# Two chained MLPs behind an attention: the column order of the MLP matmuls

## The chip, the cores and the metric

The kernel runs on one core of one Trainium2 chip. The metric is the device time of one execution in microseconds, as the median of several runs. Of one execution there is a profile with a trace of every engine: TensorE (PE; its weight loads appear as PEld), VectorE (DVE), ScalarE (ACT), GpSimd (POOL) and SyncE (SP, which issues the DMAs).

## What is computed

An attention with a learned bias over 2 batches, 8 heads, 576 positions and head dimension 64, then two MLPs over the resulting 1152 tokens of width 512, with 2048 hidden units each. The change touches the MLPs alone:

```python
# x: (1152, 512), the attention's output, token by token
h = x @ w_in                                             # 1152 x 2048
g = np.where(h > 0.0, h, np.exp(np.minimum(h, 0.0)) - 1.0)
x = g @ w_out                                            # 1152 x 512
h = x @ w2_in
g = np.maximum(h, 0.0) + np.log1p(np.exp(-np.abs(h)))
return g @ w2_out
```

## The kernel before, in words

Every operand of an MLP product is held as a high and a low part in a rounded float32 format (`F32R`), and a product is three matmuls into one accumulator: high by high, high by low, low by high.

The 1152 tokens are cut into three chunks of 512, 256 and 384 columns (`CHS`), numbered 0, 1 and 2. Each MLP goes over them in two passes (`PASSES`): chunks 0 and 1 together, then chunk 2. Inside a pass the loop runs over the 16 blocks of 128 hidden units. One block and chunk is a tile with two groups of matmuls. `ffn1` (L1137) makes h: 4 pieces of the width of 512 times 3 products, 12 matmuls into one PSUM bank, with the weights stationary and the tokens (`xh`, `xl`) as the moving operand of 512, 256 or 384 columns (the matmul is L1146). ACT and DVE then turn h into g, split in `gh` and `gl`, from the tiles that `g_tiles` (L1132) hands out. `drain` (L1173) accumulates g times the second weight matrix: in the first MLP (m = 0) the weights are stationary and g moves, 12 matmuls to a tile; in the second (m = 1) g is stationary and the 512 columns of the weights move, 3 matmuls to each 128 tokens (the matmul is L1190). The accumulators lie in PSUM for all 16 blocks (`acc`, L1126).

Over both MLPs that is 1008 matmuls with 512 moving columns (384 of `ffn1`, 192 of the first MLP's `drain`, all 432 of the second's), 576 with 384 columns and 576 with 256 columns (in both cases 384 of `ffn1` and 192 of the first MLP's `drain`): 2160 matmuls and 884,736 columns. Each has its own weight load of 128 columns.

The weights come from HBM as 64-bit floats. DMA, ACT, POOL and DVE turn them into high and low parts (L148 to L187, the last step is the low part `wl` at L187), block by block while the MLP runs. A planner (`Order`) sets the order of the instructions on every engine from written costs and due times; the tables stand in `DUE` and `ON`. It runs when the program is built, and its inputs are not touched by the change.

In SBUF all MLP operands begin at the same place within 256 bytes, but for chunk 1: its `xh` and `xl` (`x_tiles`, L111), and its g in the first MLP, are shifted by `OFF` = 48 words, which is 192 bytes, inside tiles that are 64 words longer than needed.

Of the kernel before, what the change touches and what calls it, by code (L numbers as in the profile page):

```python
# [12 lines left out]
F32R = mybir.dt.float32r  # L13
# [7 lines left out]
P = 128  # L21
# [6 lines left out]
CHS = [512, 256, 384]  # L28
# [4 lines left out]
KT = DM // P  # L33
DFF = 2048
FT = DFF // P
# [10 lines left out]
PRK = 3  # L46

NE = 5


OFF = 48

NRAW, NWB = 3, 4
NF = (3, 4)
# [57 lines left out]
def x_tiles(ctx, tc, cs, xh, xl):  # L112
    pool = ctx.enter_context(tc.tile_pool(name=f"xp{cs[0]}", bufs=1, side="right"))
    for c in cs:
        for x, nm in ((xh, "xh"), (xl, "xl")):
            if c != 1:
                x.append(pool.tile([P, KT, CHS[c]], F32R, name=f"{nm}{c}"))
            else:
                t = pool.tile([P, KT * CHS[c] + 64], F32R, name=f"{nm}{c}")
                x.append(t[:, OFF : OFF + KT * CHS[c]].rearrange("p (k n) -> p k n", k=KT))  # L120


class Weights:
# [66 lines left out]
def attention(xctx, tc, qe, qt, kt, vt, par, tab, xh, xl, W, M):  # L190
    nc = tc.nc
    ctx = ExitStack()

    x_tiles(xctx, tc, [0], xh, xl)
    vctx = ExitStack()
    vr = vctx.enter_context(tc.tile_pool(name="vr", bufs=1, side="right")).tile([P, B * HP, 9, D], F32, name="vr")
# [480 lines left out]
    for p in VPARTS:  # L677
# [3 lines left out]
        t_v += [h, lo]  # L681
    t_v += vz
    t_open = add(None, 0, lambda e: (vctx.close(), x_tiles(xctx, tc, range(1, len(CHS)), xh, xl)), t_v, 3)

    tab1 = pack_table(1)
# [408 lines left out]
    return np.concatenate(rows)  # L1094


class Mlps:


# [30 lines left out]
        return self.ps2[:, k // 2, k % 2 * CHS[c] :][:, : CHS[c]] if m == 0 else self.ps2[:, k]  # L1130

    def g_tiles(self, m, c, f):  # L1132
        tag, n, bufs = ("gs", CHS[1] + 64, 2) if c == 1 else ("g", 512, 3)
        o = OFF if c == 1 and m == 0 else 0
        return [self.ap.tile([P, n], F32R, tag=f"{tag}{x}", name=f"g{x}{m}{c}{f}", bufs=bufs)[:, o : o + CHS[c]] for x in range(2)]

    def ffn1(self, m, c, f, slot):  # L1137

        nc, xh, xl = self.nc, self.xh, self.xl
        h, l = self.W.pairs[m, f][:2]  # L1140
        ch = CHS[c]
        ps = (self.left if slot else self.right).tile([P, 512], F32, tag="ph", name=f"ph{m}{c}{f}")[:, :ch]
        n = 0
        for kk in range(KT):
            for a, x in ((h, xh[c]), (h, xl[c]), (l, xh[c])):
                nc.tensor.matmul(ps, a[:, kk], x[:, kk], start=n == 0, stop=n == 3 * KT - 1)  # L1146
                n += 1
        g, t = [], []

        def act():  # L1150
            t.append(self.ap.tile([P, DM], F32, tag="t", name=f"t{m}{c}{f}", bufs=2)[:, :ch])
            if m == 0:
                nc.scalar.activation(t[0], ps, AF.Relu, scale=-1.0)
                nc.scalar.activation(t[0], t[0], AF.Exp, scale=-1.0)
            else:
                nc.scalar.activation(t[0], ps, AF.Abs)
                nc.scalar.activation(t[0], t[0], AF.Exp, scale=-1.0)
                nc.scalar.activation(t[0], t[0], AF.Ln, bias=1.0)  # L1158

        def both():  # L1160
            if m == 0:
                nc.vector.scalar_tensor_tensor(t[0], t[0], -1.0, ps, op0=ALU.add, op1=ALU.max)  # L1162
            else:
                nc.vector.scalar_tensor_tensor(t[0], ps, 0.0, t[0], op0=ALU.max, op1=ALU.add)  # L1164

        def hi():
            g.extend(self.g_tiles(m, c, f))
            nc.scalar.copy(g[0], t[0])  # L1168

        def lo():  # L1170
            nc.vector.tensor_sub(g[1], t[0], g[0])  # L1171

        return act, both, hi, lo, g  # L1173

    def drain(self, mcf, g, parts):
        m, c, f = mcf
        gh, gl = g
        h, l = self.W.pairs[m, f][2:]
        for j in parts:
            js = slice(j * P, (j + 1) * P)  # L1180
            if m == 0:
                prods = [(a[:, js], x) for a, x in ((h, gh), (h, gl), (l, gh))]
            else:
                prods = [(a[:, js], x) for a, x in ((gh, h), (gh, l), (gl, h))]

            two = m == 0 and c == 1
            if two and f == 0 and j % 2 == 0:
                self.nc.tensor.matmul(self.ps2[:, j // 2], self.zero, self.xh[0][:, 0], start=True, stop=False)
            for n, (a, x) in enumerate(prods):
                self.nc.tensor.matmul(  # L1190
                    self.acc(m, c, j), a, x, start=f == 0 and n == 0 and not two, stop=f == FT - 1 and n == 2 and not (two and j % 2 == 0)
                )

    def finish_hi(self, c, k):
# [87 lines left out]
```

## Time and profile before

| what | value |
|---|---|
| time, median of 3 runs | 603.33 us (602.89 to 603.76) |
| the profiled execution's own time | 604.67 us |
| its span, from first to last instruction | 602.9 us |
| PE busy | 581.3 us, 96% of the span, 5165 matmuls |
| PE's weight loads busy | 495.1 us |
| DVE busy | 438.2 us, 73% |
| ACT busy | 409.7 us, 68% |
| POOL busy | 111.1 us, 18% |
| mean granted clock of TensorE | 0.982 of 2.4 GHz |

The MLP's matmuls begin at 192.2 us in the span and the last starts at 597.6 us. A matmul's duration in the trace runs from its start to the end of its results, and matmuls are pipelined, so one starts long before the one ahead of it has ended; what a matmul costs in a full stream is the distance from its start to the next one's start, not its duration. The profiled execution is 1.34 us (0.2%) above the median of the three runs, and 1.77 us of its time lie outside the span.

### The profile page before, as it was taken

How to read it: one execution, taken by the hardware profiler on the slowest of the kernel's cores; microseconds unless marked ns; L12 is line 12 of the kernel's file. 1: busy time of each engine (PE TensorE's matmuls, PEld its weight loads, DVE VectorE, ACT ScalarE, POOL GpSimd, SP SyncE). 2: the span in 40 equal slices, each digit the busy share in tenths (PEclk: the TensorE clock that was granted, in tenths of full speed). 3: DMA queues.
4: the chain of work that ended last, by engine and by line, in shares of the span. 5: the costliest groups of instructions: out<-in, count | busy, mean ns of one | idle time of the engine just before them, and what ended most of it. 6: DMA issues, size and time to landing. Idle time of an engine off the chain costs nothing.

```text
span 602.9 us, 12979 instructions
## 1 busy us (share of the span) xinstructions
PE 581.3 (96%) x5165; PEld 495.1 (82%) x5165; DVE 438.2 (73%) x883; ACT 409.7 (68%) x833; POOL 111.1 (18%) x146
## 2 busy tenths in 40 slices
PE   7778999999999999999999999999999999999996
PEld 4445777777788888888899999998888888988985
DVE  7699999999889999999943379999994232233222
ACT  6686998989998867666633476679884455455442
POOL 2322474447600011011200012100010000000000
PEclk8779999999999999999999999999999999999999
DMA  8733643244300344344530004444530000011001
GB/s 324 210 100 80 201 115 99 77 116 144 86 23 2 119 146 157 119 160 143 172 106 1 1 30 146 155 129 137 171 109 0 2 0 1 1 41 64 1 1 53
DMA packets 19069, 56.39 MB, mean 94 GB/s; under 512 B 2112, under 2 KB 2496, under 8 KB 18752
## 3 DMA queue, kind: packets, MB, share of 16 engines
q1 hardware_dynamic: 19008, 55.56, 29.4%
q8 instruction: 40, 0.66, 0.4%
q14 instruction: 21, 0.17, 0.1%
HBM read 41.40 MB, written 2.36 MB: 73 GB/s over the span
## 4 chain that ended last, share of the span: by engine, by line
PE 81%; DVE 8%; ACT 2%; issue 2%; DMA 1%; DVEq 0%; ACTq 0%
PE ps L1190 33%; PE ph L1146 33%; PE tp L564 5%; PE pb L406 4%; PE pa L589 3%; PE ps L524 3%; DVE e L534 2%; DVE et L573 2%; DVE y L399 1%; ACT sg L418 1%; DMA sp<-sg 1%; DVE wl L187 0%; PE pr L619 0%; DVE xs L607 0%; ACT e L551 0%
## 5 line engine op out<-in xcount | busy, mean ns | idle before, releaser
L1146 PE MATMUL ph<-xh,wh 128*128 128x512 f32 (+2 forms) x384 | 129.0, 336 | 0.7 <-DVE t L1162 0.7
L1146 PE MATMUL ph<-xh,wl 128*128 128x512 f32 (+2 forms) x384 | 128.8, 335 | 0.0
L1146 PE MATMUL ph<-xl,wh 128*128 128x512 f32 (+2 forms) x384 | 128.7, 335 | 0.0
L1168 ACT CAST g<-t 128x256 fp32r<-128x256 f32 (+2 forms) x96 | 48.3, 512 | 75.7 <-PE ps L1190 68.7
L1171 DVE TENSOR_TENSOR g<-t,g 128x256 fp32r<-128x256 f32 (+2 forms) x96 | 53.4, 559 | 57.4 <-ACT g L1168 57.2
L1190 PE MATMUL ps<-g,wh 128*128 128x256 f32 (+2 forms) x384 | 95.0, 335 | 0.0
L1190 PE MATMUL ps<-wh,g 128*128 128x512 f32 x288 | 94.0, 390 | 0.0
L1146 PEld LDWEIGHTS ph<-xh,wh 128*128 128x128 f32 x384 | 72.2, 188 | 7.0 <-DVE t L1162 0.9
L1146 PEld LDWEIGHTS ph<-xl,wh 128*128 128x128 f32 x384 | 72.1, 188 | 5.9
L1146 PEld LDWEIGHTS ph<-xh,wl 128*128 128x128 f32 x384 | 72.5, 189 | 5.1
L397 POOL TENSOR_SCALAR y<-tpk,nbp 128x576 f32<-128x576 f32 x71 | 61.2, 872 | 69.2 <-PE pb L406 68.7
L162 POOL TENSOR_SCALAR w<-w 128x512 f32<-128x512 f32 x36 | 30.9, 858 | 220.5 <-ACT w L154 110.9
L1190 PEld LDWEIGHTS ps<-g,wh 128*128 128x128 f32 x384 | 66.2, 188 | 4.7
L1164 DVE SCALAR_TENSOR_TENSOR t<-ph,t 128x512 f32<-128x512 f32 (+2 forms) x48 | 26.7, 555 | 54.7 <-ACT t L1158 54.5
L1190 PE MATMUL ps<-g,wl 128*128 128x512 f32 (+2 forms) x192 | 64.3, 335 | 0.0
L1190 PEld LDWEIGHTS ps<-wh,g 128*128 128x128 f32 x288 | 54.1, 188 | 10.6
L551 ACT ACTIVATE e<-e,mx 128x576 f32<-128x576 f32 x72 | 55.8, 780 | 1.7 <-DVE mx L534 1.7
L1190 PE MATMUL ps<-wl,g 128*128 128x512 f32 x144 | 56.3, 391 | 0.0
L573 DVE SCALAR_TENSOR_TENSOR et<-tp,et 128x512 f16<-128x512 f32 x81 | 53.9, 680 | 1.7 <-ACT et L568 1.6
L418 ACT ACTIVATE sg<-pb,bcst,inv 128x288 f32<-128x288 f32 x72 | 42.7, 592 | 14.9 <-PE pb L406 8.3
L568 ACT ACTIVATE et<-tp 128x512 f16<-128x512 f32 x81 | 47.0, 600 | 5.4 <-PE tp L564 4.9
L183 ACT CAST wh<-w 128x512 fp32r<-128x512 f32 x64 | 39.1, 616 | 16.5 <-DVE w L168 16.2
(115 smaller groups left out, 1047.2 us busy)
## 6 DMA issues: line engine op xcount, KB each, us to landing
r<-in_wa_dram SPq DMA_DIRECT2D x32, 512.0 KB, 3.6
r<-in_wb_dram SPq DMA_DIRECT2D x32, 512.0 KB, 3.8
bias<-sg SPq DMA_DIRECT2D x32, 288.0 KB, 3.8
kr<-in_kt_dram SPq DMA_DIRECT2D x4, 576.0 KB, 7.5
vr<-in_vt_dram SPq DMA_DIRECT2D x2, 1152.0 KB, 11.5
sp<-sg SPq DMA_DIRECT2D x8, 288.0 KB, 3.3
out_dram<-o SPq DMA_DIRECT2D x9, 256.0 KB, 2.0
qr<-in_qt_dram SPq DMA_DIRECT2D x8, 256.0 KB, 3.7
```

What stands on the lines that cost most here:

```text
L162: eng.tensor_scalar(wf, wf, F64_HUGE, F64_TINY, op0=ALU.min, op1=ALU.max)
L183: self.nc.scalar.copy(self.parts[i][0][:, x], self.words[i, x])
L397: eng.tensor_scalar(y, tpk[:, b0 : b0 + S], BIG, nbp[:, qd : qd + 1], op0=ALU.min, op1=ALU.max)
L418: nc.scalar.activation(sgs[bi, s][:, n * SH : (n + 1) * SH], pbs.pop((bi, s, n)), AF.Identity, bias=bcst, scale=inv[:, col : col + 1])
L551: nc.scalar.activation(e, e, AF.Exp, bias=mxs[u][:, x : x + 1], scale=-1.0, accum_out=sums[u - hp][:, h : h + 1])
L564: nc.tensor.transpose(tp[:, r], e[:, t * P : (t + 1) * P], ident)
L568: nc.scalar.activation(et[:, 0], tps[g, k].rearrange("p t i -> p (t i)"), AF.Copy, scale=2.0**14)
L573: nc.vector.scalar_tensor_tensor(et[:, 1], tp, 2.0**14, et[:, 0], op0=ALU.mult, op1=ALU.subtract)
L1146: nc.tensor.matmul(ps, a[:, kk], x[:, kk], start=n == 0, stop=n == 3 * KT - 1)
L1168: nc.scalar.copy(g[0], t[0])
L1171: nc.vector.tensor_sub(g[1], t[0], g[0])
L1190: self.nc.tensor.matmul(self.acc(m, c, j), a, x, start=f == 0 and n == 0 and not two, stop=f == FT - 1 and n == 2 and not (two and j % 2 == 0)
```

## The change

In every MLP matmul the columns of the moving operand and of the PSUM output are visited in another order. The new helper `in_fours` splits the column index into (a, t, b) with four values of t and of b and lets t run outermost: columns 0 to 3, 16 to 19, 32 to 35 and so on to the end, then 4 to 7, 20 to 23 and so on. A column is four bytes, so a run is 16 bytes, and the next run lies 64 bytes after the start of the last. Input and output use the same order, so each column's result lands where it did before. The shift of chunk 1 and the longer tiles are dropped: all MLP operands begin at the same place within 256 bytes.

```diff
-OFF = 48
...
-            if c != 1:
-                x.append(pool.tile([P, KT, CHS[c]], F32R, name=f"{nm}{c}"))
-            else:
-                t = pool.tile([P, KT * CHS[c] + 64], F32R, name=f"{nm}{c}")
-                x.append(t[:, OFF : OFF + KT * CHS[c]].rearrange("p (k n) -> p k n", k=KT))
+            x.append(pool.tile([P, KT, CHS[c]], F32R, name=f"{nm}{c}"))
...
+def in_fours(x):
+
+    return x.rearrange("p (a t b) -> p t a b", t=4, b=4)
...
-        tag, n, bufs = ("gs", CHS[1] + 64, 2) if c == 1 else ("g", 512, 3)
-        o = OFF if c == 1 and m == 0 else 0
-        return [self.ap.tile([P, n], F32R, tag=f"{tag}{x}", name=f"g{x}{m}{c}{f}", bufs=bufs)[:, o : o + CHS[c]] for x in range(2)]
+        tag, n, bufs = ("gs", CHS[1], 2) if c == 1 else ("g", 512, 3)
+        return [self.ap.tile([P, n], F32R, tag=f"{tag}{x}", name=f"g{x}{m}{c}{f}", bufs=bufs)[:, : CHS[c]] for x in range(2)]
...
-                nc.tensor.matmul(ps, a[:, kk], x[:, kk], start=n == 0, stop=n == 3 * KT - 1)
+                nc.tensor.matmul(in_fours(ps), a[:, kk], in_fours(x[:, kk]), start=n == 0, stop=n == 3 * KT - 1)
...
-                    self.acc(m, c, j), a, x, start=f == 0 and n == 0 and not two, stop=f == FT - 1 and n == 2 and not (two and j % 2 == 0)
+                    in_fours(self.acc(m, c, j)), a, in_fours(x), start=f == 0 and n == 0 and not two, stop=f == FT - 1 and n == 2 and not (two and j % 2 == 0)
```

No instruction of any engine changes its place. What the build adds are waits: 42 of the 96 `ffn1` groups now begin with a matmul that also waits for PE's own earlier work, and 51 of DVE's 96 steps L1162 and L1164 also wait for PE. Where a matmul waits for two engines, one of the waits becomes an instruction of its own on PE's queue.

PE near the end of the second MLP, before: the last matmuls of a `drain`, then the beginning of an `ffn1` group of chunk 2 (`ph` its bank, `ps` an accumulator, `xh` and `xl` the tokens, `wh` and `wl` the weights, `g` a part of g, with buffer numbers).

```order
L1190 MATMUL ps_68<-wh_6090,g_7768 128x512
L1190 MATMUL ps_69<-wh_6090,g_7767 128x512 [waits DVE_49]
L1190 MATMUL ps_69<-wl_6091,g_7767 128x512
L1190 MATMUL ps_69<-wh_6090,g_7768 128x512
L1146 MATMUL ph_7930<-xh_929,wh_6486 128x384 [waits DVE_49]
L1146 MATMUL ph_7930<-xl_930,wh_6486 128x384
```

The same place on PE with the change:

```order
L1187 MATMUL ps_68<-wh_6090,g_7768 128x4x32x4
L1187 MATMUL ps_69<-wh_6090,g_7767 128x4x32x4 [waits DVE_49]
L1187 MATMUL ps_69<-wl_6091,g_7767 128x4x32x4
L1187 MATMUL ps_69<-wh_6090,g_7768 128x4x32x4
L1143 MATMUL ph_7930<-xh_929,wh_6486 128x4x24x4 [waits DVE_49,PE_49]
L1143 MATMUL ph_7930<-xl_930,wh_6486 128x4x24x4
```

Nothing has moved: the shapes are now 4 by 32 by 4 and 4 by 24 by 4, and the first matmul of the `ffn1` group waits for PE beside DVE. The work on PE that it waits for, the last user of the same bank, stands 31 or more matmuls ahead of it.

## Rows read from the trace of the kernel before

**Rows 1.** Busy time of each engine by stage of the MLPs.
```profile
core 0: us, PE busy (x) PEld busy (x) DVE busy (x) ACT busy (x) POOL busy (x), PEclk, DMA share, GB/s
...
210.00:240.00 30.00, 30.00 (x181) 25.94 (x178) 29.25 (x53) 21.44 (x40) 5.31 (x6) 1.00 0.49 157
240.00:270.00 30.00, 30.00 (x174) 26.55 (x173) 27.60 (x54) 20.46 (x41) 3.64 (x4) 1.00 0.44 142
270.00:300.00 30.00, 30.00 (x174) 26.48 (x174) 28.52 (x53) 20.45 (x38) 6.87 (x8) 1.00 0.45 146
300.00:330.00 30.00, 30.00 (x197) 27.64 (x195) 12.47 (x23) 10.04 (x23) 1.48 (x2) 1.00 0.21 66
...
500.00:530.00 30.00, 30.00 (x159) 26.58 (x158) 7.51 (x14) 12.91 (x27) 0.00 (x0) 1.00 0.00 1
```

**Rows 2.** PE's own waits from 192 us to the end: all of them.
```profile
PE ph L1146 <- DVE t L1162: 0.7, 1, 0.7
```

**Rows 3.** Chain that ended last: its first and last MLP rows from 233 us on.
```profile
233.18 4.13 PE ph L1146 x24
...
585.74 11.62 PE ps L1190 x51
```

**Rows 4.** PE in order of time (start, length, both in us): 512, then 256 columns.
```profile
299.71 0.39 PE L1146 MATMUL ph<-xh,wh 128*128 128x512 f32 x1
...
302.43 0.40 PE L1190 MATMUL ps<-g,wh 128*128 128x256 f32 x2
...
303.84 0.62 PE L1190 MATMUL ps<-g,wh 128*128 128x512 f32 x2
```

**Rows 5.** PE in order of time: 384 columns.
```profile
353.72 0.33 PE L1146 MATMUL ph<-xh,wh 128*128 128x384 f32 x1
...
355.80 0.51 PE L1190 MATMUL ps<-g,wh 128*128 128x384 f32 x2
```

**Rows 6.** PE's weight loads in order of time, beside the matmuls of Rows 4.
```profile
299.71 0.19 PEld L1146 LDWEIGHTS ph<-xl,wh 128*128 128x128 f32 x1
299.94 0.19 PEld L1146 LDWEIGHTS ph<-xh,wl 128*128 128x128 f32 x1
```

**Rows 7.** Attention stage: 64-column f16 matmuls, with their weight loads.
```profile
131.71 0.58 PEld L589 LDWEIGHTS <-et 128*128 128x128 f16 x15
131.82 0.19 PE L589 MATMUL pa<-vh,et 128*128 128x64 f16 x1
...
132.20 0.19 PE L589 MATMUL pa<-vl,et 128*128 128x64 f16 x1
```

**Rows 8.** Attention stage: matmuls that read every second f16 of a row.
```profile
18.77 0.44 PE L406 MATMUL pb<-y,w2h 128*32 128x288 f16 x8
19.04 0.29 PE L406 MATMUL pb<-y,w2l 128*32 128x288 f16 x4
```

**Rows 9.** PE by form: the f32 transposes of the attention.
```profile
L564 PE MATMUL tp<-ident,e 128*128 128x128 f32 x324 | 49.3, 284 | 0.4 <-DVE et L573 0.2
```

**Rows 10.** DVE's low parts of the weights, and PE's first use of them.
```profile
256.49 0.68 DVE L187 TENSOR_TENSOR wl<-w,wh 128x512 fp32r<-128x512 f32 x1
...
258.27 0.42 PE L1146 MATMUL ph<-xh,wh 128*128 128x512 f32 x1
...
292.57 0.68 DVE L187 TENSOR_TENSOR wl<-w,wh 128x512 fp32r<-128x512 f32 x1
```

**Rows 11.** A wait as an instruction of its own on PE's queue (min/median/max ns).
```profile
L1146 PEldq EVENT_SEMAPHORE  x8: 51/51/51, 191.6 to 237.0; - x8
```

## Prediction

> **What bounds the kernel now.** I read the busy time by stage first. From 210 us on PE shows no idle time in any stage at the full clock, while DVE falls from 92 to 98% busy before 300 us to 42% after it and 25% at 500 us [rows 1]. Then PE's waits: between 192 us and the end there is one, of 0.7 us [rows 2]. The chain that ended last says the same: from 233 us on all the rows that it prints are PE's, in `ffn1` and `drain` [rows 3]. So from 233 to 597 us time is the number of matmuls times the distance of their starts, and only a change of that distance matters.
>
> The distance is not what the columns need. Twelve matmuls of 512 columns start between 299.71 and 302.43 us, 226.7 ns each; twelve of 256 columns between 302.43 and 303.84 us, 117.5 ns [rows 4]; twelve of 384 columns between 353.72 and 355.80 us, 173.3 ns [rows 5]. A column per period of 2.4 GHz would be 213.3, 106.7 and 160.0 ns. The excess is 13.4, 10.8 and 13.3 ns. It is the same at 512 and at 384 columns, so it belongs to the matmul and not to the column, and each matmul has just one other thing of fixed size beneath it: the load of the next matmul's 128 columns of f32 weights, which starts with it (299.71 beside 299.71, 299.94 beside 299.93) [rows 6]. The only width with a smaller excess is also the only one whose operands are shifted by 192 bytes. In the attention, where weights and moving operand are f16, 13 starts of 64 columns lie between 131.82 and 132.20 us: 29.2 ns against 26.7, an excess of 2.5 ns, though a weight load stands beneath each of these too [rows 7]. I read the difference, 10.9, 8.3 and 10.8 ns, as time in which the moving stream and the f32 weight load want the same part of SBUF.
>
> **The change, part by part.**
>
> *The new order of the reads.* Both streams walk through SBUF in steps of 4 bytes now; where they meet they stay together for a run of neighbouring addresses. With the new order the moving stream leaves a 64-byte stretch after 16 bytes, and it meets the weight load one run at a time. No row shows such a read of f32. From below the price is bounded by the f16 stream: 2.5 ns of excess stay, and 10.9, 8.3 and 10.8 ns go. From above by the nearest row with gaps in the moving operand, 288 columns that are every second f16: a pass of four matmuls side by side begins every 0.27/2 = 135 ns where 120 + 2.5 are needed [rows 8], so 13 ns stay, which is today's. I take the lower end, because the excess goes with the load and not with the number of columns, and because this order breaks up just the stretches in which the two can walk together. Worth: 1008 x 10.9 + 576 x 10.8 + 576 x 8.3 ns = 11.0 + 6.2 + 4.8 = 22.0 us, out of 1008 x 226.7 + 576 x 173.3 + 576 x 117.5 ns = 396.0 us, or 5.6%.
>
> *Where the cover ends.* Until 300 us PE is only just behind the weights. The low part of block 10 ends at 256.49 + 0.68 = 257.17 us and PE uses it at 258.27, 1.1 us later; that of block 15 ends at 293.25 and PE reaches it at 299.71, 6.5 us later [rows 4, 10]. DVE is 92 to 98% busy there [rows 1]. If PE gets 5.6% faster, the 90 us from 210 to 300 us shrink by 5 us, below the 85.4 us that DVE works in them (29.25 + 27.60 + 28.52) [rows 1]. The next late thing is `wl`, and I count nothing for this stage. After 300 us nothing of that kind is near: 297.6 us of matmuls x 5.6% = 16.5 us.
>
> *The order of the writes.* PSUM is written in runs of four f32 with gaps of twelve. No row shows a matmul that does so. Lower end: nothing. Upper end, far off: the slowest f32 stream here, the transposes with 49.3 us for 324 times 128 columns, 152 ns where 53 are needed [rows 9], nearly three times a column's time. I take nothing: a run is written as closely as now, and columns come no faster than now. The Trainium skill's "PSUM — Partial Sum Buffer" has a rule on it without a price (Specifications): PSUM works in lines of 8 bytes, and an access that isn't contiguous slows matmuls significantly. By its letter this change loses; by its line of two f32, which a run of four fills twice, it costs nothing. No row here shows which.
>
> *The dropped shift.* By the sizes above it is worth at most the 13.3 - 10.8 = 2.5 ns between a 256-column matmul and the others, 576 x 2.5 = 1.4 us. With the new order its reason is gone: nothing.
>
> *The added waits.* 42 `ffn1` groups also wait for the bank's last user on PE, 31 or more matmuls back, which is done. As an instruction on PE's queue a wait takes 51 ns [rows 11]: 42 x 51 ns = 2.1 us if nothing hid it, nothing if the matmuls already in PE's queue cover it, and with 117 to 227 ns to a matmul I take nothing. DVE's 51 added waits are for matmuls that ACT's step ahead of them has waited for already.
>
> *DMA, ACT, POOL.* No instruction moves, and the queues have room: DMA is at most 49% busy in these stages, ACT at most 71% [rows 1]. The tail after the last matmul stays.
>
> Sum: 604.67 - 16.5 = 588.2 us for the profiled execution, which stands 1.34 us above the median of the runs; against the median, 603.33 - 16.5 = **586.8 us**.
>
> **The rivals.**
>
> *Half of it stays* (15%). Two streams that meet more often but more briefly may lose as many periods. For it: the 135 ns of the attention's gapped reads [rows 8], though there four matmuls share the array. Half of 16.5 is 8.2 us: 595.1 us.
>
> *The excess has nothing to do with addresses* (10%). Then it stays, and the time is 603.3 us, or up to 2 us more if waits show. For it: it hardly depends on where an operand lies, 10.8 to 13.4 ns. Against it: the f16 stream with loads beneath it has 2.5 [rows 7]. The Trainium skill's "TensorE: Matmul & The Clock Gate" (Part 2, step 1) speaks for this rival: it says that PE has two independent SBUF read ports, so that loading the next weights doesn't take read bandwidth from the running matmul. By that rule nothing is to be gained; the rows with and without f32 loads speak the other way, which is why I leave it at one in ten.
>
> *Only the shift is lost* (8%). The order changes nothing and chunk 1 gets the excess of the others: + 1.4 us, and up to 2.1 us for the waits: 604.7 to 606.8 us.
>
> *Runs cost PE time* (17%), the other side. The place is PSUM's accumulation: if a run of four that doesn't follow on the last one costs a period, 884,736 / 4 = 221,184 runs x 0.42 ns = 92 us come on top of the forecast: 679 us. It decides from 16.5 us / 221,184 = 75 ps to a run, under a fifth of a period, so the slightest regular cost makes the change lose. For it: the trace has an f32 stream at nearly three times a column's time [rows 9], and no row of a write with gaps. Against it: a run is four columns in four periods with no gap inside, as now. The rule of the Trainium skill's "PSUM — Partial Sum Buffer" above, by its letter, is this rival.
>
> **How the numbers follow.** A measurement of this kernel tells 0.2%, 1.2 us, from no change. The forecast, most of the excess gone, has 50%, with a range of its own from 581 us (all 22.0 us, also before 300 us) to 592 us (two thirds of the 16.5). Faster: 50 + 15 = 65%. Same: 10%. Slower: 8 + 17 = 25%. The range leaves out the costly runs and reaches over the small loss: 581 to 606 us.
>
> **What would show it.** Right: 512, 384 and 256 columns start every 216, 162 to 163 and 109 to 110 ns after 300 us; PE has some new waits for DVE or its weights between 210 and 300 us, a few us in all; the tail is as now. Half right: distances of 221 and 168 ns. Wrong: the same 227 and 173 ns, or 256 columns at 120; and if the distance grows in proportion to the columns (512 more than 384 by a third) the runs cost, not the loads. If PE's start distances shrink and the time doesn't, the weights have become the bound in the first MLP.

## The result and the profile after

The changed kernel takes 598.44 us in the median of 6 runs (596.66 to 599.11), beside 603.55 us (602.89 to 604.00, 6 runs) before. The ratio is 0.9911, with a 95% interval from 0.9894 to 0.9928: faster by 5.1 us, where 16.5 were forecast. The profiled execution took 597.05 us, its span is 595.2 us. The two profiled executions lie further apart than the medians, 7.6 us (604.67 and 597.05); 1.8 us of that lie ahead of the MLP stage, where the change touches nothing: the stage begins at 192.2 us before and at 190.4 after. Direction and bound were right; the size was not.

The page's first section and its costliest groups, of the changed kernel (busy time in us, mean ns of one instruction, idle time before it):

```profile
PE 575.4 (97%) x5165; PEld 491.6 (83%) x5165; DVE 437.8 (74%) x883; ACT 410.8 (69%) x833; POOL 111.0 (19%) x146
...
L1143 PE MATMUL ph<-xh,wh 128*128 128x512 f32 (+2 forms) x384 | 127.5, 332 | 0.9 <-DVE t L1159 0.8
L1143 PE MATMUL ph<-xl,wh 128*128 128x512 f32 (+2 forms) x384 | 126.9, 330 | 0.0
```

The same two groups stood at 129.0 and 128.7 us, so they are 1.2% and 1.4% shorter in busy time; what the kernel gains is in the distances of the starts, below. DVE, ACT and POOL are busy within about 1 us of what they were. The stages that answer to [rows 1]:

```profile
core 0: us, PE busy (x) PEld busy (x) DVE busy (x) ACT busy (x) POOL busy (x), PEclk, DMA share, GB/s
210.00:240.00 30.00, 30.00 (x165) 26.11 (x164) 29.31 (x55) 22.16 (x41) 6.71 (x6) 1.00 0.44 148
...
270.00:300.00 30.00, 30.00 (x172) 26.47 (x171) 29.12 (x52) 19.55 (x36) 5.93 (x8) 1.00 0.46 159
...
500.00:530.00 30.00, 30.00 (x157) 26.83 (x156) 7.59 (x14) 13.90 (x30) 0.00 (x0) 1.00 0.00 1
```

PE is still without idle time at the full clock. Its own waits from 185 us to the end (one, the same as before), and two rows of the chain, answer to [rows 2, 3]:

```profile
PE ph L1143 <- DVE t L1159: 0.8, 1, 0.8
```
```profile
329.11 12.15 PE ph L1143 x72
...
578.13 11.56 PE ps L1187 x51
```

So the bound is what it was, and the time went where the prediction looked for it, into the distance of the starts. PE in order of time: of twelve with 512 columns the first and the seventh to the eleventh, then the first of twelve with 256 columns and the matmul behind these twelve, then the same for 384:

```profile
296.78 0.39 PE L1143 MATMUL ph<-xh,wh 128*128 128x512 f32 x1
...
298.14 0.38 PE L1143 MATMUL ph<-xh,wh 128*128 128x512 f32 x1
298.36 0.38 PE L1143 MATMUL ph<-xl,wh 128*128 128x512 f32 x1
298.58 0.39 PE L1143 MATMUL ph<-xh,wl 128*128 128x512 f32 x1
298.81 0.39 PE L1143 MATMUL ph<-xh,wh 128*128 128x512 f32 x1
299.04 0.38 PE L1143 MATMUL ph<-xl,wh 128*128 128x512 f32 x1
...
299.48 0.39 PE L1187 MATMUL ps<-g,wh 128*128 128x256 f32 x2
...
300.83 0.61 PE L1187 MATMUL ps<-g,wh 128*128 128x512 f32 x2
...
349.96 0.33 PE L1143 MATMUL ph<-xh,wh 128*128 128x384 f32 x1
...
352.00 0.51 PE L1187 MATMUL ps<-g,wh 128*128 128x384 f32 x2
```

Twelve of 512 columns: (299.48 - 296.78)/12 = 225.0 ns, where 226.7 stood in [rows 4] and 216 was forecast. Twelve of 256: (300.83 - 299.48)/12 = 112.5, before 117.5. Twelve of 384: (352.00 - 349.96)/12 = 170.0, before 173.3 in [rows 5]. The steps are no longer even: from the start at 298.14 on they are 224, 221, 218 and 230 ns (the trace has the starts to the nanosecond, the rows to 10 ns), where the twelve of [rows 4] are all 226 or 227.

A single group of twelve is a small sample, so from here on a distance is the mean over the whole MLP stage of the starts of one width, without those more than 40 ns above the columns' own time; the stage runs from the start of its first matmul to that of its last. Each such number comes from one trace. The changed kernel traced a second time gives 115.0, 170.2 and 225.0 ns and a stage of 400.44 us, so less than 1 ns or 1 us between two traces tells nothing. A kernel's time below is of one execution, but for the changed kernel (6), the shift dropped alone (8, with 11 of the kernel before beside it), the order with the shift kept (4) and the version beyond the change (6).

| kernel | 256 | 384 | 512 columns, ns | stage, us |
|---|---|---|---|---|
| columns' own time at 2.4 GHz | 106.7 | 160.0 | 213.3 | |
| before | 117.1 | 174.2 | 227.6 | 405.41 |
| after | 114.9 | 170.2 | 224.4 | 399.53 |

1008 x 3.2 + 576 x 4.0 + 576 x 2.2 ns are 6.8 us. The stage is 5.9 us shorter: the distances left out of the means add 0.9 us more than before, nearly all at five places after 255 us, where an `ffn1` group begins. The longest of them, PE and then DVE in order of time:

```profile
380.50 0.33 PE L1187 MATMUL ps<-g,wl 128*128 128x384 f32 x1
380.94 0.41 PE L1143 MATMUL ph<-xh,wh 128*128 128x384 f32 x1
```
```profile
380.25 0.55 DVE L1159 SCALAR_TENSOR_TENSOR t<-t,ph 128x384 f32<-128x384 f32 x1
```

Here 440 ns lie between two starts, 270 more than usual: DVE reads `ph` until 380.25 + 0.55 = 380.80, and only then a new group begins. Of the 5.9 us, 1.0 falls on the first 100 us of the stage: the same `ffn1` group begins 292.85 - 192.23 = 100.6 us into it before, and 290.02 - 190.43 = 99.6 after.

The waits that the build added are there, as instructions on PE's queue at the line of `ffn1` (min/median/max ns):

```profile
L1143 PEldq EVENT_SEMAPHORE  x50: 51/51/51, 189.8 to 575.2; - x50
```

[Rows 11] had 8 of them, so 42 are new. The distances in which they lie are the usual ones to 11 ns, but for one: an instruction at 380.83 us, in the 440 ns above, where PE waits for DVE in any case.

### The profile page after: what moved, and what is told of

Same layout as the page of the kernel before. It is cut to its first block, busy times and chain, and to the rows that moved or that the text cites. A ratio compares the mean times of both kernels' runs of the same rounds, so it can differ in the third digit from the quotient of the medians.

```text
span 595.2 us, 13058 instructions
## 1 busy us (share of the span) xinstructions
PE 575.4 (97%) x5165; PEld 491.6 (83%) x5165; DVE 437.8 (74%) x883; ACT 410.8 (69%) x833; POOL 111.0 (19%) x146
## 4 chain that ended last, share of the span: by engine, by line
PE 81%; DVE 8%; issue 2%; ACT 2%; DMA 1%; DVEq 0%; ACTq 0%
PE ps L1187 33%; PE ph L1143 33%; PE tp L557 5%; PE pb L399 4%; PE ps L517 4%; PE pa L582 3%; DVE e L527 2%; DVE et L566 2%; DVE y L392 1%; ACT sg L411 1%; DMA sp<-sg 1%; DVE wl L180 0%; PE pr L612 0%; DVE xs L600 0%; ACT e L544 0%
## 5 line engine op out<-in xcount | busy, mean ns | idle before, releaser
L1143 PE MATMUL ph<-xh,wh 128*128 128x512 f32 (+2 forms) x384 | 127.5, 332 | 0.9 <-DVE t L1159 0.8
L1143 PE MATMUL ph<-xl,wh 128*128 128x512 f32 (+2 forms) x384 | 126.9, 330 | 0.0
L1143 PE MATMUL ph<-xh,wl 128*128 128x512 f32 (+2 forms) x384 | 126.8, 330 | 0.0
L1187 PE MATMUL ps<-wh,g 128*128 128x512 f32 x288 | 92.7, 385 | 0.0
L1161 DVE SCALAR_TENSOR_TENSOR t<-ph,t 128x512 f32<-128x512 f32 (+2 forms) x48 | 26.7, 556 | 53.9 <-ACT t L1155 53.7
L147 ACT ACTIVATE w<-r 128x512 f32<-128x512 f32 x64 | 45.1, 709 | 11.9 <-DMA r<-in_wb_dram 8.0
```

Source lines behind the costliest of these rows:

```text
L147: self.nc.scalar.activation(w.bitcast(F32), self.raws[i, x][:, :, 1].bitcast(F32), AF.Abs)
L1143: nc.tensor.matmul(in_fours(ps), a[:, kk], in_fours(x[:, kk]), start=n == 0, stop=n == 3 * KT - 1)
L1187: self.nc.tensor.matmul(in_fours(self.acc(m, c, j)), a, in_fours(x), start=f == 0 and n == 0 and not two, stop=f == FT - 1 and n == 2 and ...
```

## The experiments

In the expectations, theory 1 is the prediction's reading: the excess is the moving stream meeting the f32 weight load beneath it. Theory 2 puts the excess into the moving stream alone, whatever is loaded: first as a fixed price for each matmul, later (2a) as a price of its walk through SBUF. The diffs are against the changed kernel unless they say otherwise.

### Which part of the change counts

*The shift dropped, nothing else.*
```diff
-    return x.rearrange("p (a t b) -> p t a b", t=4, b=4)
+    return x
```


> The old order of columns, only the 192-byte shift of chunk 1 is gone. Theory 1 (the excess is the moving stream meeting the f32 weight load, and the order of the reads decides how they meet): 512 and 384 columns stay at 226.7 and 173.3 ns from start to start, 256 columns go from 117.5 to between 117.5 and 120 ns; 0 to 1.4 us slower than before. Rival (the shift was a cost and dropping it is the gain): 256 columns fall to about 115 ns and the time falls by 1 us or more.

*The order with the shift kept* (the removed lines on `OFF` put back).


> The new order of columns with the shift of chunk 1 kept. Theory 1: 512 and 384 columns as in the changed kernel, 224 and 170 ns on average; 256 columns 114 to 116 ns; the time within 1 us of the changed kernel's 598.4 us. Rival (the gain comes with equal places within 256 bytes): 256 columns stay at 117.5 ns, about 1.5 us slower than the changed kernel.

*The order on the reads alone:* the results land in other columns.
```diff
-nc.tensor.matmul(in_fours(ps), a[:, kk], in_fours(x[:, kk]), ...
+nc.tensor.matmul(ps, a[:, kk], in_fours(x[:, kk]), ...
...
-    in_fours(self.acc(m, c, j)), a, in_fours(x), ...
+    self.acc(m, c, j), a, in_fours(x), ...
```


> The moving columns are read in the new order, but PSUM is written in the old, one after the other; the results then lie in other columns. Theory 1: the reads do all of it, so the mean distances are those of the changed kernel, 224, 170 and 115 ns. Rival 2 (the gapped PSUM writes give back part of a larger gain from the reads): 216 to 220 ns at 512 columns and 163 to 166 at 384.

*The order on the PSUM writes alone:* the same two lines, with `in_fours` on the output only.


> PSUM is written in the new order, the moving columns are read in the old; the results lie in other columns. Theory 1: 226.7, 173.3 and 117.5 to 120 ns as before the change, writes cost nothing. Rival 2 (gapped writes cost): more than 227 and 173 ns, by about 4 to 8 ns.

| kernel | 256 | 384 | 512, ns | stage, us | time, us | before beside it |
|---|---|---|---|---|---|---|
| shift dropped alone | 119.5 | 174.1 | 228.3 | 407.50 | 606.57 | 604.59 |
| order, shift kept | 114.4 | 169.8 | 225.1 | 399.88 | 599.50 | 604.59 |
| reads alone | 114.9 | 169.9 | 225.0 | 399.61 | 599.23 | 604.59 |
| writes alone | 119.5 | 174.1 | 228.3 | 407.47 | 607.03 | 604.59 |

Dropping the shift alone makes the kernel slower, 1.0039 (1.0025 to 1.0054): 2.4 ns on each 256-column matmul. The order with the shift kept gives 0.9914 (0.9886 to 0.9942), the whole of the change. With the writes alone the distances are those of the dropped shift to a tenth of a nanosecond, so runs of four in PSUM, 64 bytes from one to the next, cost nothing; with the reads alone they are those of the changed kernel. The kernel with the reads alone has 8 of the waits on PE's queue and not 50, and on DVE's, for the steps L1159 and L1161, 47 as before the change and not 82; its stage is as long as the changed kernel's, 399.61 and 399.53 us: the added waits cost nothing that can be measured. PE in order of time, writes alone, twelve of 256, twelve of 512 and the next:

```profile
299.21 0.28 PE L1143 MATMUL ph<-xh,wh 128*128 128x256 f32 x1
...
300.64 0.40 PE L1143 MATMUL ph<-xh,wh 128*128 128x512 f32 x1
...
303.39 0.40 PE L1187 MATMUL ps<-g,wh 128*128 128x256 f32 x2
```

119.2 and 229.2 ns. The same view with the reads alone:

```profile
297.55 0.27 PE L1143 MATMUL ph<-xh,wh 128*128 128x256 f32 x1
...
298.94 0.39 PE L1143 MATMUL ph<-xh,wh 128*128 128x512 f32 x1
...
301.63 0.39 PE L1187 MATMUL ps<-g,wh 128*128 128x256 f32 x2
```

115.8 and 224.2 ns. The reads carry the change.

### Whether the weight load beneath makes the excess

*Loads of 64 columns instead of 128*, in the old order (against the kernel before) and in the new one. The first and the last matmul of an `ffn1` group, and blocks 0 and 15 of `drain`, keep whole loads; the others compute half of their output rows. With 4 columns they compute 4 rows, so these runs shrink the load and the output together; the moving operand stays whole.
```diff
+k_ = P if n in (0, 3 * KT - 1) else 64
-nc.tensor.matmul(ps, a[:, kk], x[:, kk], ...
+nc.tensor.matmul(ps[:k_], a[:, kk, :k_], x[:, kk], ...
...
-    self.acc(m, c, j), a, x, ...
+    self.acc(m, c, j)[: P if f in (0, FT - 1) else 64], a[:, : P if f in (0, FT - 1) else 64], x, ...
```


> The kernel before, but all MLP matmuls except the first and last of an ffn1 group and those of the first and last block of a drain use only 64 of the 128 stationary columns, so half of every other weight load and of the sums is left out. Theory 1 (the excess over the columns' own time comes from the f32 load beneath): the excess of 13.4 ns falls to 2.5 + 5.4 = about 8 ns: 221 ns at 512 columns, 168 at 384. Rival 3 (the excess has nothing to do with the load): 226.7 and 173.3 ns stay.

> The changed kernel with the same half loads. Theory 1: what the new order leaves, 11.1 ns at 512 columns and 10.2 at 384 against the columns' own time, halves beyond the 2.5 ns of the f16 stream: about 219.6 and 166 ns. Rival 3: 224.4 and 170.2 ns stay.

*Loads of 4 columns*: the same edit with 4 for 64, in the old order, in the new one, and with every eighth run (see below).


> The kernel before, but all MLP matmuls except the first and last of an ffn1 group and those of the first and last block of a drain load only 4 stationary columns (16 bytes of a row), so most of the sums is left out. Theory 1 (the moving stream meets the f32 weight load): with next to no load beneath, 215.8 ns at 512 columns and 162.5 at 384. Theory 2 (the moving stream loses the time alone, at a fixed price for each matmul): 226.7 and 173.3 ns stay.

> The changed kernel with the same loads of 4 columns. Theory 1: 215.8 and 162.5 ns. Theory 2: about 224 and 170 ns, as in the changed kernel. With half loads the means were 222.9 and 167.0 ns.

> Runs of four, every eighth run first, with loads of 4 columns. With full loads this order took 244.9 ns at 512 columns and 182.9 at 384, an excess of about 6% of the columns. Theory 1: 215.8 and 162.5 ns, for the excess is the meeting with the load. Theory 2: 245 and 183 ns stay, for the stream is slow by itself in steps of 128 bytes.

*A heavier load*: the weights' columns in steps of 16 bytes, against the kernel before, in `ffn1` and in the first MLP's `drain`.
```diff
-nc.tensor.matmul(ps, a[:, kk], x[:, kk], ...
+nc.tensor.matmul(ps, a.rearrange("p k f -> p (k f)")[:, kk::KT], x[:, kk], ...
...
-prods = [(a[:, js], x) for ...
+prods = [(a[:, j::KT], x) for ...
```


> The kernel before, but the 128 stationary columns of ffn1 and of the first MLP's drain are every fourth word of a row of 512, so that a load touches four times as many 16-byte pieces; the products are of other columns. The second MLP's drain is as before. Theory 1: more meetings, the distances of ffn1 rise clearly over 226.7 and 173.3 ns (by 10 ns or more), while those of the second MLP's drain stay at 227 where a drain matmul loads for the next. Theory 2: 226.7 and 173.3 ns everywhere.

| kernel | 256 | 384 | 512, ns | stage, us | time, us |
|---|---|---|---|---|---|
| old order, loads of 64 | 117.5 | 173.9 | 230.0 | 407.77 | 606.62 |
| old order, loads of 4 | 114.4 | 174.6 | 231.2 | 407.58 | 606.84 |
| new order, loads of 64 | 113.8 | 167.0 | 222.9 | 397.02 | 595.59 |
| new order, loads of 4 | 113.0 | 169.7 | 223.2 | 397.57 | 596.64 |

PE's weight loads in order of time, old order with loads of 4, and under them PE itself:

```profile
300.14 0.19 PEld L1147 LDWEIGHTS ph<-xh,wh 128*128 128x128 f32 x1
300.25 0.08 PEld L1147 LDWEIGHTS ph<-xl,wh 128*4 128x4 f32 x1
300.48 0.09 PEld L1147 LDWEIGHTS ph<-xh,wl 128*4 128x4 f32 x1
```
```profile
300.25 0.40 PE L1147 MATMUL ph<-xh,wh 128*128 128x512 f32 x1
300.48 0.40 PE L1147 MATMUL ph<-xl,wh 128*4 128x512 f32 x1
...
303.03 0.39 PE L1191 MATMUL ps<-g,wh 128*4 128x256 f32 x2
```

The load is down from 0.19 to 0.08 us and reads a 32nd of the columns, and the distance is (303.03 - 300.25)/12 = 231.7 ns, 5 more than before. Theory 1 wanted it near 216. What the load adds is seen in the new order, where smaller loads save 0.5 to 3.2 ns a matmul, and at 256 columns in the old order, where loads of 4 save 2.7; at 512 columns in the old order they even cost some. In the old order with loads of 4 the excess over the columns' own time is 7.7, 14.6 and 17.9 ns at 256, 384 and 512 columns: it does grow with the columns, and the fixed price of theory 2 missed too. Traffic of DVE and DMA is not behind it either: before the change the starts of 512 columns are mostly 226 or 227 ns apart between 500 and 530 us as well, where DVE is busy for 25% of the time and DMA moves next to nothing [rows 1].

With the heavier load the 512-column matmuls of `ffn1` rise to a median of 237 ns and the second MLP's `drain` stays at 227, as theory 1 had it, but for another reason. Loads took about 0.32 us there and came one every 235 ns, so they set the pace themselves, at every width (PE in order of time, twelve of 256 columns):

```profile
331.01 0.52 PE L1190 MATMUL ps<-g,wh 128*128 128x256 f32 x2
...
333.72 0.75 PE L1190 MATMUL ps<-g,wh 128*128 128x512 f32 x2
```

That is 225.8 ns for 256 columns. The time was 710.63 us. Of what a load does to a moving stream that is slower than it, this run says nothing.

### What the step of the walk costs

The moving operand keeps its runs of 16 bytes; the step from one run to the next is changed from 64 bytes to 32, 128 and 256, and once runs of 64 bytes are taken in steps of 256.
```diff
-    return x.rearrange("p (a t b) -> p t a b", t=4, b=4)
+    return x.rearrange("p (a t b) -> p t a b", t=8, b=4)
```
(t = 2 for every second run, 16 for every sixteenth; t = 4, b = 16 for the longer runs.)


> Runs of four columns, every eighth run first: steps of 128 bytes instead of 64. Theory 1, if only the length of the stretch in which the streams walk together counts: as the changed kernel, 224 and 170 ns. If the place within 256 bytes counts (a 128-byte step visits two quarters of it, not four): other distances, up to the 227 and 173 ns of before or beyond.

> Runs of sixteen columns (64 bytes), every fourth run first: steps of 256 bytes. If the length of the walk together counts: as before the change, 227 and 173 ns, since a run is as long as a 64-byte stretch. If the place within 256 bytes counts: other distances, since the stream stays in one quarter of it for a quarter of the matmul.

> Runs of four, every second run first: steps of 32 bytes. Theory 2a with parts of SBUF that change every 64 bytes: two pieces in a row from the same part, between the old order's four and the new order's one, so 224.4 to 227.6 ns at 512 columns. With parts that change every 32 bytes: every piece from another part, fewer than 224 ns. With no dependence but the step's length: between the old order and the new.

> Runs of four, every sixteenth run first: steps of 256 bytes. Theory 2a with a period of 256 bytes or less: all pieces of a sweep from the same part, at least as slow as steps of 128 bytes, 245 ns or more at 512 columns and 183 or more at 384. If only the length of a step counts against the stream: slower than 245 by a clear amount.

| run, step in bytes | 256 | 384 | 512, ns | time, us |
|---|---|---|---|---|
| 16, 16 (shift dropped alone) | 119.5 | 174.1 | 228.3 | 606.57 |
| 16, 32 | 117.8 | 174.5 | 233.2 | 609.03 |
| 16, 64 (the change) | 114.9 | 170.2 | 224.4 | 598.44 |
| 16, 128 | 121.2 | 182.9 | 246.3 | 630.86 |
| 16, 256 (medians) | 135.3 | 206 | 278 | 683.50 |
| 64, 256 | 118.3 | 178.6 | 239.1 | 619.03 |

(The 40 ns limit doesn't fit the two slowest steps: at 128 bytes 133 plain distances of 512 columns lie beyond it, so the 512-column mean goes up to 60 ns there, and at 256 bytes medians stand.)

PE in order of time, every sixteenth run: twelve of 512 columns in `ffn1`, twelve in `drain`, twelve of 256 in `ffn1`:

```profile
291.03 0.45 PE L1143 MATMUL ph<-xh,wh 128*128 128x512 f32 x1
...
294.36 0.72 PE L1187 MATMUL ps<-g,wh 128*128 128x512 f32 x2
...
297.67 0.31 PE L1143 MATMUL ph<-xh,wh 128*128 128x256 f32 x1
...
299.31 0.43 PE L1187 MATMUL ps<-g,wh 128*128 128x256 f32 x2
```

277.5, 275.8 and 136.7 ns. Same bytes, same columns, same loads: with the step the 512-column matmul moves between 224 and 278 ns, and not in one direction. Among the steps tried 64 bytes is the best. The 32-byte step is slower than the plain order at 512 columns and met none of its three expectations. At 128 and 256 bytes the excess goes with the columns (14.5, 22.9, 33.0 and 28.6, 46, 65 ns), and with loads of 4 columns the 128-byte step stays at 117.6, 180.9 and 245.0 ns (627.80 us): the load isn't what makes it slow. One thing is left open: `in_fours` stands on the PSUM output too, so the step of the writes changed together with that of the reads. That the writes cost nothing was shown for 64 bytes alone; at 32, 128 and 256 bytes the two were not separated.

### Whether it is the number of bytes walked

*bfloat16 in the old order, every second value:* both operands are the upper halves of the f32 words, so the moving operand walks the same bytes with the same columns, and rounding is coarser (shift kept).
*bfloat16 packed:* the same stationary operand, the moving one a constant row of 512 values side by side, so that the MLPs compute something else. Both against the kernel before.
```diff
+def moving(x):
+    return x.bitcast(BF16)[:, 1::2]
...
-nc.tensor.matmul(ps, a[:, kk], x[:, kk], ...
+nc.tensor.matmul(ps, still(a[:, kk]), moving(x[:, kk]), ...
...
-    self.acc(m, c, j), a, x, ...
+    self.acc(m, c, j), still(a), moving(x), ...
```
(`still` does the same for the weights; in the second kernel `self.mv[:, : CHS[c]]`, a constant bfloat16 tile, stands for `moving(...)`.)


> The kernel before with both operands of every MLP matmul read as bf16, the upper half of each word: four columns to 16 bytes as in f32, but a 2-byte type and its faster weight loads; the lower halves of all values are left out of the products. Theory 2a (the moving stream pays for every 16-byte piece of SBUF that it opens): the same number of pieces, so an excess of 8 ns or more over the columns' own time stays, 222 ns or more at 512 columns. Theory 2b (the price is that of f32 as a type, in the loads or in the array): 215.8 and 162.5 ns.

> As the run above, but the moving operand is one packed bf16 tile of a constant, eight columns to 16 bytes; the tokens, g and the moving weights are left out of the products. Theory 2a: half as many pieces at the same rate of columns, and as in the f16 matmuls of the attention only 2.5 ns stay: 215.8 ns at 512 columns, 162.5 at 384. If 227 and 173 ns stay here too, neither type nor pieces matter, and the price belongs to a matmul with a load of its own in such a stream.

| kernel | 256 | 384 | 512, ns | stage, us | time, us |
|---|---|---|---|---|---|
| every second | 113.4 | 168.9 | 225.1 | 397.64 | 596.69 |
| packed | 109.2 | 162.5 | 215.8 | 388.92 | 589.26 |

PE in order of time, every second value, twelve of 512 columns:

```profile
291.10 0.39 PE L1156 MATMUL ph<-xh,wh 128*128 128x512 bf16 x1
...
293.80 0.61 PE L1200 MATMUL ps<-g,wh 128*128 128x512 bf16 x2
```

That is 225.0 ns. The same for packed values, twelve of 256 columns, twelve of 512 and the next:

```profile
296.58 0.38 PE L1153 MATMUL ph<-mv,wh 128*128 128x256 bf16 x2
...
297.89 0.59 PE L1153 MATMUL ph<-mv,wh 128*128 128x512 bf16 x2
...
300.48 0.38 PE L1197 MATMUL ps<-mv,wh 128*128 128x256 bf16 x2
```

Every distance is the columns' own time plus 2.5 ns: the floor that [rows 7] gave. Every second value, with the same kind of load (96 and 98 ns), has 113.4, 168.9 and 225.1. Beyond the floor that is 4.2, 6.4 and 9.3 ns, where f32 has 7.9, 11.7 and 11.8 before the change: the walk over four bytes for each column keeps a good half of the excess at 256 and 384 columns and most of it at 512, with two bytes side by side nothing is left, and the rest goes with the f32 type in a way that no run takes apart. (The packed operand is also one constant tile; that its address and its values never change was not separated from the packing.)

The packed kernel also has PE at the floor that the forecast described, so it shows what becomes late then, with one limit: its moving operand waits for nothing, so what would come late in the tokens, in the first `drain`'s g or in the second `drain`'s weights doesn't show in it. PE's own waits in the packed kernel, from 200 us on:

```profile
PE ph L1153 <- DVE t L1169: 2.4, 5, 0.9
PE ph L1153 <- DVE t L1171: 2.1, 3, 1.0
```

4.5 us of waits for DVE's reads of `ph`, after which `ffn1` may write a bank again; 3.0 of them lie after 300 us.

### A version beyond the change

*The attention too:* `in_fours` on input and output of the scores (L517, 288 columns of four bytes) and of the bias matmuls (L399, 288 columns, every second f16), with the changed kernel beside it in the same rounds.
```diff
-pb[32 * c : 32 * c + 32],
+in_fours(pb[32 * c : 32 * c + 32]),
...
-ps_of(x)[:, n], q[r], k[r, n * SH : (n + 1) * SH], ...
+in_fours(ps_of(x)[:, n]), q[r], in_fours(k[r, n * SH : (n + 1) * SH]), ...
```


> The changed kernel, with the attention's scores (288 columns of four bytes) and bias matmuls (288 columns, every second f16) also visited by every fourth run of four. Theory (each 16-byte piece of the moving operand has a price that the step to the next piece sets, and 64 bytes is a better step than 16): the score passes, 131.9 ns now where 122.5 would do, fall to 128 to 130 ns, the bias passes from 133.8 likewise; 240 score and 216 bias passes by 3 ns are 1.4 us where PE sets the pace, so 597.0 to 598.5 us. Rival (four row or column tiles that share the array hide the price, or the attention waits for other engines): the passes stay at 132 and 134 ns, or they fall and the time stays at 598.4 us.

> The changed kernel once more, on the same chip as the one above: 598.4 us, 0.991 of the kernel before. No theory expects another time; it gives the pair for the version above.

Before took 604.18 us there; the version 598.67 us, 0.9915 (0.9900 to 0.9931), the changed kernel 597.69 us, 0.9893 (0.9876 to 0.9910). The intervals overlap, so it is no gain. Of the distances from one pass to the next, those between 115 and 150 ns have a mean of 130.6 ns for the scores, 131.9 in the changed kernel beside it, and of 132.3 for the bias, 131.8 beside it: a miss for the 3 ns expected. Both passes have several matmuls side by side, and the MLP's gain doesn't carry over to them; why was not tested. No version tried that computes the same beats the change.

## Why the prediction was wrong

**The bound: right.** PE sets the time from 210 us on before and after, and the time moved with the distances: in the profiled pair 6.8 us from them, 0.9 given back, and 5.1 us between the medians.

**The step that failed is the order of the reads.** "I read the difference ... as time in which the moving stream and the f32 weight load want the same part of SBUF", and from it the lower end. With loads of 4 columns the 512-column distance is 231.2 ns, not near 216: the load was a companion of the excess, not its cause. So the term of 10.9, 10.8 and 8.3 ns a matmul, 22.0 us in all, came to 3.2, 4.0 and 2.2 ns, 6.8 us. Two arguments led there. "It is the same at 512 and at 384 columns, so it belongs to the matmul": 13.4 and 13.3 ns, but 17.9 and 14.6 with loads of 4 columns, and 15.0, 14.1 and 12.8 ns at 512, 384 and 256 with the shift dropped alone, so that two widths agreed was an accident, and part of what set the third apart was its shift. And [rows 7], the f16 stream with loads beneath it, differs from the MLP in two things at once, the load's type and the moving operand's bytes for each column; I named the first. The Trainium skill's "TensorE: Matmul & The Clock Gate" (Part 2, step 1) says that loading the next weights takes no read bandwidth from the running matmul; the runs with loads of 4 columns agree with it, but for 0.5 to 1.9 ns in the new order and 2.7 ns at 256 columns in the old. The rival that it spoke for had one in ten and was half right: the load is not the cause, but addresses matter all the same.

**What stood in its place.** Most of the excess belongs to the moving stream's own walk: it stays without the load, moves with the order of the reads alone, and is gone with packed values. The change picks a better step for this walk, not a stream without excess: beyond the floor of 2.5 ns, 11.8 - 3.2 = 8.6 ns of the 512-column excess stay. Had the nearer row for a gapped read [rows 8] been taken, the sum would have been none. The truth lies between the bounds, and I took an end. Why the walk costs what it does stays open.

**The floor and the cover: the floor exists, the cover is about as thick as summed, but not where it was put.** The change never came to either; only the packed kernel, which reads something else, did. It starts its matmuls at 215.8, 162.5 and 109.2 ns, where 216, 162 to 163 and 109 to 110 were forecast for the change, and takes 589.26 us where 588.2 were summed; some of that agreement is luck, as its distances save more and it waits more. Its distances would save 1008 x 11.8 + 576 x 11.7 + 576 x 7.9 = 23.2 us, and its stage is 16.5 us shorter. Of the 6.7 us between, 6.3 are longer distances of the kind shown above at 380.50 us, the 4.5 us of waits for DVE among them. So about as much was taken back as the forecast had left out, 5.5 us of 22.0, but not where it said: the waits that PE has are for a bank of `ph` and none for `wl`, and more than half comes after 300 us. At the changed kernel's pace there is little of this, 0.9 us.

**The writes: right.** Nothing, by the kernel that changes the writes alone. The costly-runs rival (679 us, 17%) fell with it. This holds for the 64-byte step. The Trainium skill's "PSUM — Partial Sum Buffer" (Specifications), that an access which isn't contiguous slows matmuls significantly, is not borne out for runs of four f32 with gaps of twelve: 228.3 ns with gaps and without.

**The dropped shift: right.** 2.4 ns for a 256-column matmul in the old order, where at most 2.5 were allowed; with the new order 114.9 without it and 114.4 with it.

**The added waits: right.** All 42 stand on PE's queue and some more on DVE's, and the kernel with the reads alone, which has none of the added ones, is not faster: 399.61 us of stage beside 399.53.

**The rivals.** The one that came nearest is "half of it stays" (595.1 us), with the wrong reason; nearer still would have been "two thirds stay", which I didn't list. The range, 581 to 606 us, held the time, because it reached to the case of no change.

## What to carry to other kernels

Two rows that differ in two things don't tell which of them costs; before building a sum on one, look for the row, or make the run, that differs in it alone (here a load of 4 columns). In a stream bound by PE with four bytes to a column, the order in which the moving columns are walked is worth some per cent, and far more downwards: try the step, since against plain order steps of 32, 64, 128 and 256 bytes gave 2% more, 2% less, 8% more and 22% more at 512 columns, in no order that follows from the step's size. Where the arithmetic allows packed two-byte values, the one packed kernel here did better than every order of four-byte ones that was tried.

## What the runs showed of the hardware

- A 512-column matmul whose moving operand has four bytes to a column begins every 224 to 278 ns by the step between its 16-byte runs (of reads and PSUM writes together, but at 64 bytes, where it is the reads); packed two-byte columns begin every 215.8 ns. The Trainium skill's "SBUF — State Buffer" (Specifications) gives 16-byte lines, full bandwidth from two hits to a line, and a penalty for each crossing to a new line. Here every line gets four hits, and the plain order still loses 11.8 ns of a 512-column matmul beyond the floor. A penalty for each crossing fits that, but one fixed price doesn't: with steps of 16 to 256 bytes the crossings are as many, and the distances are not the same. Why 64 bytes are better than 16, 32 and 128 stays open.
- In long stretches of the new order the starts of 512 columns follow a pattern of four, 230, 224, 221 and 218 ns; three in four of the old order's are 226 or 227 ns. What repeats in it stays open.
- A weight load of 128 f32 columns takes 0.19 us, of 64 columns 0.13, of 4 columns 0.08. In steps of 16 bytes, 128 columns take 0.32 us, come every 235 ns and set the pace of the matmuls: the walk of the stationary operand matters too.
- PSUM takes runs of four f32 with gaps of twelve at the pace of a plain row, 228.3 ns at 512 columns either way.
